# Regrouping the PSUM banks and moving small VectorE work in a fused attention and feed-forward kernel

## The chip, the cores and the metric

The kernel runs on one core of a Trainium2 chip. The metric is the device time of one launch in microseconds (us). The kernel before takes 555.98 us, the median of nine runs (555.08 to 556.79).

The engines are TensorE (PE in the profile; its weight loads have a row of their own, PEld), VectorE (DVE), ScalarE (ACT), GpSimd (POOL) and SyncE (SP, which here only issues transfers). TensorE writes its results to PSUM, which this kernel divides into eight banks of 512 fp32 columns on 128 partitions. DVE and ACT bring them from there to SBUF.

## The reference

The inputs are q, k and v of 8 batches, 12 heads, 448 tokens and 64 dimensions, a gain g of 768, and the weights w1 (768 x 3072) and w2 (3072 x 768).

```
scores = q @ k.T / sqrt(64)
attn   = max(scores, 0)**2 / 448
x      = attn @ v                       # 8 x 448 x 768 after the heads are joined
mu, var over the 768 columns
xn     = (x - mu) / sqrt(var + 1e-6) * g
out    = x + max(xn @ w1, 0) @ w2       # float32
```

## The kernel before

**Order of work.** The order of every engine's queue is the order of the program text (`tc.manual_schedule`), so what stands ahead of an instruction in the text on the same engine also runs ahead of it. First comes the attention of batch 0 (`step_fine`, `first_end`). Then, for each batch, `ffn_1_all(b)` (24 tiles of 128 hidden columns, `ffn_1`) and FFN2: `ffn_2_first` for batch 0, `ffn_2_all` for the others. The attention of batch b + 1 is woven into the feed-forward of batch b: in FFN1 of batch 0 by `step_a` and `step_b` at every second tile, afterwards by `excursion`, which takes three score slots of work at each tile of `IN_FFN1` (the AV product of a finished pair of heads, three times QK with ReLU, three squares), and by `between` inside FFN2.

**Attention.** `att_T` makes the transposes of q and k of a pair of heads, on TensorE for batches 0 and 1, by transfers later. `att_QK` multiplies k by q for the two heads of a pair (two matmuls with 64 rows each, one per half of a two-bank slot) and applies the ReLU: ACT for most, DVE for the third one of an excursion (`relus=(2,)`, L229). `att_square` squares on DVE (L236). `att_AV` (L250) multiplies by v into one bank, which L260 (DVE) or L258 (ACT) empties into xT.

**Mean and gain.** LayerNorm is applied as xc = g x - g mean, and the division by the standard deviation comes at the end. `gain` (L276, ACT) makes g x; `center` makes the mean with four matmuls (L282), two on xs (the sum of the first five column blocks) and two on the last block of xT, and subtracts it with six DVE instructions (L288).

**FFN1.** `ffn_1` runs twelve matmuls into one of two f banks (`next_f` gives them in turn, also to AV in FFN1), and ACT applies the ReLU into h (L324). `h` holds 640 columns: the 448 of this batch at the right (from CARRY = 192), and to their left the tokens that the batch before left over, because FFN2 works on pairs of 128-token tiles. `carry(b)` (L336, DVE) copies these leftover columns from the right end of h to the left, after the last pair. From tile 16 or 18 on, `ffn_stats` computes mean and variance of a token tile on DVE at every second tile.

**FFN2.** Batch 0 multiplies two token tiles plainly (`plain_part`, L370), with four output pieces in turn in the f banks; after each, DVE writes the scaled result (`scaled_plus`, L356). The other batches use Strassen's seven products for each pair of tiles (`seven`, L387): products c, d, a, c, d, a, and c again, in three banks. With `s_sb` (L381) DVE forms the sums of h, with `w2_sums` (L178) the sums of w2, in two halves each. `flush` emits the evacuations of a product after the next product. Batches 1, 2, 3, 5, 6 and 7 have two pairs, batch 4 has one; with one pair the first bank is z, with two it is x and z is the second.

**PSUM before.** Three slots of two banks (`sc`) and two f banks. One score slot is always held back from the turns: slot 0 in the attention of batch 0 (warm-up matmuls and the third tile of `ffn_1_first` in one bank, the first mean in the other), and in FFN2 the slot that has been unused longest, whose halves are the bank z and the bank for AV. In FFN1 all three turn; the TensorE transposes from pair 7 on and the mean of `center` take a half of the next slot.

```
x_bank = f_turn.items[0]
y_bank = f_turn.items[1]
z_bank, av_bank = hold[:, 0], hold[:, 1]
...
banks = [x_bank, z_bank, y_bank] if len(pairs) == 2 else [z_bank, x_bank, y_bank]
```

Of the kernel before, what the change touches and what calls it, by code (L numbers as in the profile page):

```python
# [11 lines left out]
def kernel(  # L12
# [10 lines left out]
    nc = tc.nc  # L23
    P = 128
# [3 lines left out]
    Alu = mybir.AluOpType  # L28
# [55 lines left out]
    v_ring = big_pool.tile([SP, NPAIR, 2, NJ * D], bf16)  # L84

    sc = []
    for n in range(3):
        sc_t = ps_pool.tile([P, 2, 512], fp32, name=f"sc{n}")
        sc.append(sc_t)
    fb = []  # L90
    for n in range(2):
        f_t = ps_pool.tile([P, 512], fp32, name=f"f{n}")
        fb.append(f_t)

# [3 lines left out]
    class Turns:  # L98
        def __init__(self, items):
            self.items = list(items)  # L100

        def next(self, skip=()):
            n = next(n for n, it in enumerate(self.items) if not any(it is s for s in skip))
            it = self.items.pop(n)
            self.items.append(it)
            return it

    sc_turn = Turns(sc)
    f_turn = Turns(fb)
    held = [sc[0]]  # L110

    def next_sc():
        return sc_turn.next(held)

    next_f = f_turn.next

    PE_T = 2
    EARLY = H * NJ * D
# [81 lines left out]
    def att_T(i, copy=None):  # L200
        if i >= PE_T * NPAIR:
            new_qkT(i)
            for t in range(2):
                nc.sync.dma_start_transpose(
                    qkT[i][:, t, :].rearrange("p (j s) -> p j s", j=NJ), qk_ring[:, i % 3, t])
            return
        if i == 0:
            new_qkT(0)
            for t, cp in enumerate((nc.vector.tensor_copy, nc.scalar.copy)):
                ps = bf_view(next_f())  # L210
                pe_T(0, t, ps)
                cp(qkT[0][:, t, :], ps[:, t, :])
            return
        ps = bf_view(next_f() if i <= NPAIR else next_sc()[:, 0])
        for t in range(2):
            pe_T(i, t, ps)
        new_qkT(i)
        (copy or nc.vector.tensor_copy)(qkT[i], ps)  # L218

    def att_QK(i, t, square=True, relu_by=None):  # L220
        at = attn_pool.tile([SP, 2, S], bf16, tag="attn")
        attn[i, t] = at
        ps = next_sc()
        for hh in range(2):
            r = slice(hh * D, (hh + 1) * D)
            nc.tensor.matmul(ps[:SP, hh, :S], qkT[i][r, 1, t * SP:(t + 1) * SP], qkT[i][r, 0, :],  # L226
                             start=True, stop=True)
        if relu_by is nc.vector:
            nc.vector.tensor_scalar(at, ps[:SP, :, :S], 0.0, None, op0=Alu.max)  # L229
        else:  # L230
            nc.scalar.activation(at, ps[:SP, :, :S], Act.Relu)  # L231
        if square:
            att_square(i, t)
# [33 lines left out]
        elif 1 < pr < NPAIR - 1:  # L267
            nc.vector.tensor_add(xs, xs, xT_of(b, pr))

    mean0 = sc[0][:, 1, :S]  # L270

    def mean_part(ki):
        nc.tensor.matmul(mean0, ones, xT_of(0, ki), start=(ki == 0), stop=(ki == K1 - 1))
# [2 lines left out]
        nc.scalar.activation(xc[:, ki, :], xT_of(b, ki), Act.Identity, scale=g_sb[:, ki:ki + 1])  # L276

    def center(b):
        mean_ps = next_sc()[:, 0, :S]
        for n, part in enumerate((xs, xT_of(b, K1 - 1))):  # L280
            for c in range(2):
                nc.tensor.matmul(mean_ps[c * D:(c + 1) * D, :], ones[:, :D], part,  # L282
                                 start=(n == 0), stop=(n == 1))
        for ki in range(K1):
            center_part(ki, mean_ps)
# [37 lines left out]
                                 start=(ki == 0), stop=(ki == K1 - 1))  # L323
        nc.scalar.activation(h[:, ni, CARRY:], ps, Act.Relu)  # L324


    done_to = [0]

    def h_cols(b, m):
        c0 = CARRY + m * P - b * S  # L330
        return slice(c0, c0 + P)

    def carry(b):
        n = (b + 1) * S - done_to[0] * P
        if n:
            nc.vector.tensor_copy(h[:, :, CARRY - n:CARRY], h[:, :, HW - n:])  # L336

    def new_o():
        o_t = o_pool.tile([P, HD], fp32, tag="o")
# [58 lines left out]
    def seven(b, pair, banks, last, between):  # L398
# [63 lines left out]
            between(n)  # L462
        if last:
            cut = HD - P
            parts = ((bb, 0, cut), (sc[0][:, 1], cut, HD))
            for ps, d0, d1 in parts:
                product(ps, sums[6], B_TOP, True, d0, d1)
                flush()

                def after(ps=ps, d0=d0, d1=d1):  # L470
                    o_t = new_o()[:, :d1 - d0]
                    scaled_plus(o_t, ps[:, :d1 - d0], m2, acc2[:, d0:d1])
                    store(o_t, m2, HD + d0, HD + d1, (nc.sync, nc.scalar))
                posts.append(after)
            flush()

    def warm_up(n):
        for _ in range(n):
            nc.tensor.matmul(sc[0][:, 0, :256], ones, warm, start=True, stop=True)

    NP_ALL = B * NPAIR

# [79 lines left out]

    def ffn_1_first():
        f_ps, m_ps = next_f(), next_f()
        tiles = [t[:, :S] for t in (f_ps, m_ps, sc[0][:, 0])]
        for ki in range(K1):
            center_part(ki, mean0)
            for ni, ps in enumerate(tiles):
                nc.tensor.matmul(ps, w1[:, ki, ni * P:(ni + 1) * P], xc[:, ki, :],  # L569
                                 start=(ki == 0), stop=(ki == K1 - 1))  # L570
        for ni, ps in enumerate(tiles):
            nc.scalar.activation(h[:, ni, CARRY:], ps, Act.Relu)
        for t in range(2):
            att_square(NPAIR, t)
        held.clear()

    def second_steps():
        yield lambda: step_b(NPAIR)
# [4 lines left out]
    def ffn_1_all(b):  # L583
        steps = second_steps() if b == 0 else None
        ms = tiles_of(b)
        for ni in range(3 if b == 0 else 0, K2):
            if b == 0 and ni == 3:
                ffn_1_first()
            if 3 <= ni < 3 + K1:
                ffn_x(b, ni - 3)  # L590
            ffn_1(ni)
            flush()
            m = (ni - (K2 - 2 * len(ms))) // 2
            if m >= 0 and ni % 2 == 0:
                ffn_stats(ms[m])
            if b == 1 and ni in (1, 3):
                w2_sums(B12, B12, B22, Alu.subtract, ni // 2)
                w2_sums(B21, B21, B11, Alu.subtract, ni // 2)
            if b == 0 and ni % 2 == 1:
                next(steps)()  # L600
            if 0 < b < B - 1 and ni in IN_FFN1[b]:
                excursion(3, relus=(2,))
        assert steps is None or next(steps, None) is None

    ONE = [b for b in range(B) if ((b + 1) * S // (2 * P)) - (b * S // (2 * P)) == 1]
    IN_FFN1 = {b: (1, 4, 7, 10, 13, 16, 19, 22) if b in ONE else (2, 5, 8, 11, 14, 17, 20)
               for b in range(B)}

    def ffn_2_first():
        b = 0  # L610
        ffn_rstd(b)
        box = {}
        n = 0
        for dh in range(2):
            for m in range(2):
                for part in range(4):
                    plain_part(b, m, dh, part, 4, box)
                    if n == 1:
                        att_AV(PE_T * NPAIR - 1)
                    if n < K1 - 1:  # L620
                        gain(1, n)
                    if n == 3:
                        gain(1, K1 - 1)
                    if n == 4:
                        gain(1, K1 - 2)
                        center(1)
                    if n >= 9 and n < 15:
                        slot, x, y = ((B_SUM, B11, B22), (B_TOP, B11, B12), (B_BOT, B21, B22))[(n - 9) // 2]
                        w2_sums(slot, x, y, Alu.add, (n - 9) % 2)
                    n += 1  # L630
        done_to[0] = 2
        carry(b)

    def ffn_2_all(b):
        ffn_rstd(b)
        hold = sc_turn.items[0]
        held.append(hold)
        x_bank = f_turn.items[0]
        y_bank = f_turn.items[1]
        z_bank, av_bank = hold[:, 0], hold[:, 1]  # L640
        first = done_to[0] // 2
        pairs = range(first, (b + 1) * S // (2 * P))
        banks = [x_bank, z_bank, y_bank] if len(pairs) == 2 else [z_bank, x_bank, y_bank]
        gains = list(range(K1)) if b < B - 1 else []
# [1 line left out]

        def between(n):
            n += 7 * (pr - first)
            if b == B - 1:
                return  # L650
            if slots_left():
                if n in (1, 3):
                    excursion(min(2, slots_left()), av_bank, nc.scalar)
            elif ready:
                att_AV(ready.pop(0), bank=av_bank, evac_by=nc.scalar)
            done = (b + 2) * NPAIR - len(ready) - NPAIR * (b + 1)
            done -= sum(1 for i, t in slots if t == NJ - 1 and i < (b + 2) * NPAIR)
            for _ in range(2):
                if gains and gains[0] < done:
                    gain(b + 1, gains.pop(0))  # L660
            if not gains and not centered[0]:
                center(b + 1)
                centered[0] = True
# [4 lines left out]
        for pr in pairs:  # L668
            last = b == B - 1 and pr == pairs[-1]
            seven(b, pr, banks, last, between)  # L670
            banks = banks[1:] + banks[:1]
            if pr == pairs[-1]:
                done_to[0] = 2 * (pairs[-1] + 1)
                carry(b)
        assert centered[0] and not gains
        held.clear()

    E = mybir.EngineType
    ENGINES = [E.PE, E.Pool, E.DVE, E.Activation, E.SP]
# [62 lines left out]
```

## Time and profile before

| | |
|---|---|
| median of nine runs | 555.98 us |
| the profiled execution | 555.8 us, its span 553.8 us |
| DVE L336, the carry copies | 6 instructions, 5.7 us |
| DVE L178, the sums of w2 | 10 instructions, 13.0 us, mean 1353 ns |
| DVE L229, ReLU of the third score | 43 instructions, 46.8 us, mean 1088 ns |
| DVE L260, emptying AV | 37 instructions, 22.8 us, mean 617 ns |
| TensorE L226, the scores | 384 matmuls, 54.6 us |

The span is the time from the first to the last instruction of one profiled execution; the time of the execution holds some 2.0 us more. In the lines of the timeline the columns are the start, the duration, the engine, the line of the kernel, the operation, the tile written and the tile read, their shapes, and how many instructions are merged; in brackets stands the idle time of the engine before it, with what released it. A row of the waits has the engine, the tile and line that waited, what it waited for, the total in us, how many times, and the longest. Matmul ends are modelled, so the distance from one start to the next says more than a duration.

The stages in this execution: attention of batch 0 to 42 us, FFN1 of batch 0 to 80, its FFN2 to 98, FFN1 of batch 1 to 136, its FFN2 to 168, and so on; FFN2 of batch 4 lies between 341.5 and 358.5 us.

### The profile page before, as it was taken

To read this page: it belongs to the slowest core of one execution; us is meant where nothing else is said; L and a number is where in the kernel's file an instruction comes from. 1 tells how busy PE (TensorE), PEld (TensorE's weight loads), DVE (VectorE), ACT (ScalarE), POOL (GpSimd) and SP (SyncE) were. 2 spreads that over 40 slices of the span, in tenths; PEclk is the share of its full clock that TensorE was granted. 3 is DMA by queue.
4 is the path that set the end of the run, shared out by engine and by line. 5 is a ranking of instruction groups with operands and counts; after the bars stand their busy time and mean duration, and the time that the engine had idled before them with its cause. 6 is when DMAs were issued, how large, how long until landed. Compare 5 with 4: busy or idle time off the path is not lost. (4 is left out here: it accounts for less than half of the span.)

```text
span 553.8 us, 13597 instructions
## 1 busy us (share of the span) xinstructions
PE 531.8 (96%) x5729; PEld 342.4 (62%) x5729; DVE 398.7 (72%) x677; ACT 265.9 (48%) x421; POOL 143.9 (26%) x208
## 2 busy tenths in 40 slices
PE   8969999899999999999999999899999999999996
PEld 5425557555676556855568555655568556687785
DVE  4954577979885788847887569857897677960475
ACT  6926781466405664056640665276630766204400
POOL 8222147027400643015520228104720000000000
PEclk9978999999999999999999999999999999999999
DMA  9999999269733985449962479529963310122022
GB/s 165 196 189 207 204 161 163 51 88 118 78 71 84 113 81 61 86 88 106 91 72 83 70 87 122 74 66 94 118 82 84 71 28 2 54 65 52 5 59 58
DMA packets 162988, 51.86 MB, mean 94 GB/s; under 512 B 128752, under 2 KB 162928, under 8 KB 162928
## 3 DMA queue, kind: packets, MB, share of 16 engines
q0 software_dynamic: 94176, 25.74, 49.5%
q1 hardware_dynamic: 68256, 24.86, 22.6%
q8 instruction: 45, 0.74, 0.6%
q10 hardware_dynamic: 496, 0.40, 0.2%
q14 instruction: 15, 0.12, 0.1%
HBM read 51.91 MB, written 11.01 MB: 114 GB/s over the span
## 5 line engine op out<-in xcount | busy, mean ns | idle before, releaser
L322 PE MATMUL f<-xc,w 128*64 128x448 bf16 x2268 | 227.5, 355 | 1.9 <-DVE o_t L356 1.3
L322 PEld LDWEIGHTS <-w 128*64 128x64 bf16 x2268 | 130.5, 110 | 90.8 <-issue 19.8
L324 ACT ACTIVATE h<-f 128x448 bf16<-128x448 f32 x189 | 103.1, 546 | 165.6 <-PE f L322 149.6
L231 ACT ACTIVATE at<-sc 112x896 bf16<-112x896 f32 x149 | 128.1, 916 | 20.1 <-PE sc L226 20.1
L387 PEld LDWEIGHTS <-s_sb 128*64 128x64 bf16 x1584 | 103.6, 110 | 26.1 <-DVE s_sb L381 2.2
L236 DVE TENSOR_TENSOR at<-at 112x896 bf16<-112x896 bf16 x192 | 110.3, 619 | 13.1 <-ACT at L231 12.9
L138 POOL DMA_DIRECT2D qk_ring<-in_q_dram x72 | 50.7, 710 | 218.0 <-DMA qkT_t<-qk_ring 196.9
L387 PE MATMUL f<-w,s_sb 128*64 128x384 bf16 x1080 | 93.0, 326 | 1.2 <-DVE s_sb L381 1.2
L229 DVE TENSOR_SCALAR at<-sc 112x896 bf16<-112x896 f32 x43 | 46.8, 1088 | 27.1 <-PE sc L226 26.9
L381 DVE TENSOR_TENSOR s_sb<-h 128x1536 bf16<-128x1536 bf16 x65 | 60.6, 949 | 0.0
L138 POOL DMA_DIRECT2D qk_ring<-in_k_dram x72 | 50.3, 703 | 20.8 <-DMA w<-in_moe_w_ch_dram 11.3
L226 PE MATMUL sc<-qkT_t 64*112 64x448 bf16 x384 | 54.6, 369 | 0.3 <-DVE qkT_t L218 0.2
L387 PEld LDWEIGHTS <-h 128*64 128x64 bf16 x624 | 40.1, 110 | 16.2 <-issue 5.5
L260 DVE TENSOR_SCALAR xT<-f 128x448 bf16<-128x448 f32 x37 | 22.8, 617 | 34.6 <-PE f L250 21.6
L387 PE MATMUL sc<-w,s_sb 128*64 128x384 bf16 (+2 forms) x504 | 42.9, 319 | 0.2 <-DVE s_sb L381 0.2
L226 PEld LDWEIGHTS <-qkT_t 64*112 64x112 bf16 x384 | 20.0, 125 | 31.9 <-issue 27.2
L288 DVE SCALAR_TENSOR_TENSOR xc<-sc,g_sb,xc 128x448 bf16<-128x448 f32 x48 | 29.6, 680 | 8.3 <-PE sc L569 5.7
L387 PE MATMUL sc<-w,h 128*64 128x384 bf16 x312 | 27.7, 326 | 4.3 <-DVE o_t L356 4.3
L250 PE MATMUL f<-at,v_ring 112*64 112x448 bf16 x248 | 30.0, 355 | 0.0
L387 PE MATMUL f<-w,h 128*64 128x384 bf16 x312 | 27.7, 326 | 0.0
L250 PEld LDWEIGHTS <-v_ring 112*64 112x64 bf16 x336 | 18.2, 109 | 13.4 <-issue 2.9
L276 ACT ACTIVATE xc<-xT,g_sb 128x448 bf16<-128x448 bf16 x43 | 26.2, 667 | 0.4 <-DVE xT L260 0.2
(71 smaller groups left out, 315.7 us busy)
## 6 DMA issues: line engine op xcount, KB each, us to landing
w<-in_moe_w_ch_dram POOLq DMA_DIRECT2D x6, 768.0 KB, 30.9
w<-in_moe_w_ch_dram POOLq DMA_DIRECT2D x4, 1152.0 KB, 36.4
qk_ring<-in_q_dram POOLq DMA_DIRECT2D x72, 56.0 KB, 3.4
qk_ring<-in_k_dram POOLq DMA_DIRECT2D x72, 56.0 KB, 3.8
v_ring<-in_v_dram POOLq DMA_DIRECT2D x36, 112.0 KB, 3.8
out_dram<-o_t SPq DMA_DIRECT2D x9, 168.0 KB, 2.5
out_dram<-o_t SPq DMA_DIRECT2D x9, 144.0 KB, 2.1
x_tok<-xT SPq DMA_TRANSPOSE x72, 2.5
```

The lines of the kernel that those rows point to most:

```text
L138: nc.gpsimd.dma_start(sb[:, :, x, :], src[b, 2 * a + x].rearrange("(p j) d -> p j d", j=NJ))
L226: nc.tensor.matmul(ps[:SP, hh, :S], qkT[i][r, 1, t * SP:(t + 1) * SP], qkT[i][r, 0, :], start=True, stop=True)
L229: nc.vector.tensor_scalar(at, ps[:SP, :, :S], 0.0, None, op0=Alu.max)
L231: nc.scalar.activation(at, ps[:SP, :, :S], Act.Relu)
L236: nc.vector.tensor_mul(attn[i, t], attn[i, t], attn[i, t])
L250: nc.tensor.matmul(ps[hh * D:(hh + 1) * D, :], v_of(i)[:, hh, t * D:(t + 1) * D], attn[i, t][:, hh, :], start=(t == 0), stop=(t == NJ - 1))
L276: nc.scalar.activation(xc[:, ki, :], xT_of(b, ki), Act.Identity, scale=g_sb[:, ki:ki + 1])
L288: nc.vector.scalar_tensor_tensor(xc[:, ki, :], mean_ps, g_sb[:, ki:ki + 1], xc[:, ki, :], op0=Alu.mult, op1=Alu.add)
L322: nc.tensor.matmul(ps[c * D:(c + 1) * D, :], w1[:, ki, n0:n0 + D], xc[:, ki, :], start=(ki == 0), stop=(ki == K1 - 1))
L324: nc.scalar.activation(h[:, ni, CARRY:], ps, Act.Relu)
L381: nc.vector.tensor_tensor(s_sb[:, n], x, y, op=op)
L387: nc.tensor.matmul(ps[c * D:(c + 1) * D, :d1 - d0], stat[:, ki, c * D:(c + 1) * D], w2[:, slot, ki, d0:d1], start=(start and ki == 0), sto ...
```

## The change

PSUM becomes two slots of two banks (sc) and four single banks: two f banks as before, and two more, `spare`. Where DVE applies the ReLU, the scores of the two heads go to spare[0] and spare[1], and DVE reads them with two instructions. The transposes of `att_T` from pair 7 on take the spare banks in turn. The first mean is in spare[0]; the warm-up matmuls, the third tile of `ffn_1_first`, the mean of `center` and the last cut of the last product are in spare[1]; AV within `ffn_2_first` is in spare[0]. In `ffn_2_all`, z is spare[0] and the bank for AV is spare[1], and no slot is held back.

The carry copy is made in two halves of h and inside FFN2: in batch 0 after the ninth of sixteen parts (n = 8), in two-pair batches after the second product of the second pair (n = 8), in batch 4 after the second product (n = 1). The sums of w2: `ffn_2_first` keeps B_SUM (n = 9 and 10) and B_TOP (n = 12 and 13, before at 11 and 12); B_BOT, which stood there at n = 13 and 14, and B12 and B21, which stood at tiles 1 and 3 of FFN1 of batch 1, go to tiles 0, 3, 6, 9, 12 and 15 of it, one half each.

```diff
-    for n in range(3):
+    for n in range(2):
         sc_t = ps_pool.tile([P, 2, 512], fp32, name=f"sc{n}")
...
-    for n in range(2):
+    for n in range(4):
         f_t = ps_pool.tile([P, 512], fp32, name=f"f{n}")
...
+    next_sc = Turns(sc).next
+    f_turn = Turns(fb[:2])
     next_f = f_turn.next
+    spare = fb[2:]
+    next_spare = Turns(spare).next
...
-        ps = bf_view(next_f() if i <= NPAIR else next_sc()[:, 0])
+        ps = bf_view(next_f() if i <= NPAIR else next_spare())
...
-        ps = next_sc()
+        ps = next_sc() if relu_by is not nc.vector else None
         for hh in range(2):
             r = slice(hh * D, (hh + 1) * D)
-            nc.tensor.matmul(ps[:SP, hh, :S], qkT[i][r, 1, t * SP:(t + 1) * SP], qkT[i][r, 0, :],
+            half = spare[hh] if ps is None else ps[:, hh]
+            nc.tensor.matmul(half[:SP, :S], qkT[i][r, 1, t * SP:(t + 1) * SP], qkT[i][r, 0, :],
                              start=True, stop=True)
-        if relu_by is nc.vector:
-            nc.vector.tensor_scalar(at, ps[:SP, :, :S], 0.0, None, op0=Alu.max)
+        if ps is None:
+            for hh in range(2):
+                nc.vector.tensor_scalar(at[:, hh], spare[hh][:SP, :S], 0.0, None, op0=Alu.max)
...
-    mean0 = sc[0][:, 1, :S]
+    mean0 = spare[0][:, :S]
...
-        mean_ps = next_sc()[:, 0, :S]
+        mean_ps = spare[1][:, :S]
...
     def carry(b):
-        n = (b + 1) * S - done_to[0] * P
-        if n:
-            nc.vector.tensor_copy(h[:, :, CARRY - n:CARRY], h[:, :, HW - n:])
+        n = (b + 1) * S % (2 * P)
+        for k0 in range(0, K2 if n else 0, KH):
+            nc.vector.tensor_copy(h[:, k0:k0 + KH, CARRY - n:CARRY], h[:, k0:k0 + KH, HW - n:])
...
-            parts = ((bb, 0, cut), (sc[0][:, 1], cut, HD))
+            parts = ((bb, 0, cut), (spare[1], cut, HD))
...
-            nc.tensor.matmul(sc[0][:, 0, :256], ones, warm, start=True, stop=True)
+            nc.tensor.matmul(spare[1][:, :256], ones, warm, start=True, stop=True)
...
-        tiles = [t[:, :S] for t in (f_ps, m_ps, sc[0][:, 0])]
+        tiles = [t[:, :S] for t in (f_ps, m_ps, spare[1])]
...
-            if b == 1 and ni in (1, 3):
-                w2_sums(B12, B12, B22, Alu.subtract, ni // 2)
-                w2_sums(B21, B21, B11, Alu.subtract, ni // 2)
+            if b == 1 and ni in SUMS_AT:
+                w2_sums(*LATE_SUMS[SUMS_AT.index(ni)])
...
+    SUMS_AT = (0, 3, 6, 9, 12, 15)
+    LATE_SUMS = [(o, x, y, op, part)
+                 for o, x, y, op in ((B_BOT, B21, B22, Alu.add), (B12, B12, B22, Alu.subtract),
+                                     (B21, B21, B11, Alu.subtract)) for part in range(2)]
...
-                        att_AV(PE_T * NPAIR - 1)
+                        att_AV(PE_T * NPAIR - 1, bank=spare[0])
...
-                    if n >= 9 and n < 15:
-                        slot, x, y = ((B_SUM, B11, B22), (B_TOP, B11, B12), (B_BOT, B21, B22))[(n - 9) // 2]
-                        w2_sums(slot, x, y, Alu.add, (n - 9) % 2)
+                    if n == 8:
+                        carry(b)
+                    if n in (9, 10):
+                        w2_sums(B_SUM, B11, B22, Alu.add, n - 9)
+                    if n in (12, 13):
+                        w2_sums(B_TOP, B11, B12, Alu.add, n - 12)
                     n += 1
-        done_to[0] = 2
-        carry(b)
...
-        hold = sc_turn.items[0]
-        held.append(hold)
-        x_bank = f_turn.items[0]
-        y_bank = f_turn.items[1]
-        z_bank, av_bank = hold[:, 0], hold[:, 1]
-        first = done_to[0] // 2
+        x_bank, y_bank = f_turn.items
+        z_bank, av_bank = spare
+        first = b * S // (2 * P)
...
             n += 7 * (pr - first)
+            if n == (8 if len(pairs) == 2 else 1):
+                carry(b)
...
-            if pr == pairs[-1]:
-                done_to[0] = 2 * (pairs[-1] + 1)
-                carry(b)
```

More of the change, by code (lines that the diff above doesn't have):

```diff
@@ L100, in __init__, with next @@
             self.items = list(items)
-        def next(self, skip=()):
-            n = next(n for n, it in enumerate(self.items) if not any(it is s for s in skip))
-            it = self.items.pop(n)
+        def next(self):
+            it = self.items.pop(0)
             self.items.append(it)
             return it
[L108 to L113, printed above, removed]
+    next_sc = Turns(sc).next
+    f_turn = Turns(fb[:2])
     next_f = f_turn.next
+    spare = fb[2:]
+    next_spare = Turns(spare).next
     PE_T = 2
@@ L324, in ffn_1 @@
         nc.scalar.activation(h[:, ni, CARRY:], ps, Act.Relu)
-    done_to = [0]
     def h_cols(b, m):
@@ L574, in ffn_1_first @@
             att_square(NPAIR, t)
-        held.clear()
     def second_steps():
@@ L671, in ffn_2_all @@
             banks = banks[1:] + banks[:1]
-            if pr == pairs[-1]:
-                done_to[0] = 2 * (pairs[-1] + 1)
-                carry(b)
         assert centered[0] and not gains
-        held.clear()
     E = mybir.EngineType
```

## The prediction

> **What bounds it.** I read the page first, then what TensorE waits for, then the timeline around each of those waits.
>
> ```profile
> PE 531.8 (96%) x5729; PEld 342.4 (62%) x5729; DVE 398.7 (72%) x677; ACT 265.9 (48%) x421; POOL 143.9 (26%) x208
> ...
> PE sc L387 <- DVE o_t L356: 4.3, 5, 0.9
> PE sc L282 <- ACT xT L258: 2.2, 5, 0.4
> PE f L322 <- DVE o_t L356: 1.3, 1, 1.3
> ...
> PE f L370 <- DVE o_t L356: 0.7, 1, 0.7
> PE f L322 <- ACT h L324: 0.6, 1, 0.6
> ```
>
> TensorE is busy for 96% of the 553.8 us span, and the change takes no matmul away. So only TensorE's waits can be won or added, and the rows above are the ones that the change touches: three single waits around 85 to 102 us (the end of batch 0) and two that come once in each of the five FFN2 stages with two pairs and a centring (batches 1, 2, 3, 5, 6). VectorE (DVE) at 72% matters only where it is late for TensorE.
>
> I count from start to start, because ends overlap. Twelve L322 matmuls (one ffn_1 tile) take 36 x 0.0978 / 3 = 1.17 us (three tiles run 3.52 in the chain), 24 of L370 or L387 take 1.95, and a DVE instruction holds its engine about 0.08 less than its duration: four weight sums of 1.353 start at 94.59 and the next instruction at 99.66, so 1.27 each.
>
> **End of batch 0: the gain.** In the timeline:
>
> ```profile
> 85.65 1.17 PE L370 MATMUL f<-w,h 128*64 128x384 bf16 x12 [0.71 <-DVE o_t L356]
> ...
> 94.59 5.16 DVE L178 TENSOR_TENSOR w<-w 128x2304 bf16<-128x2304 bf16 x4
> 97.72 1.33 PE L322 MATMUL f<-xc,w 128*64 128x448 bf16 x12
> 99.66 0.61 DVE L356 SCALAR_TENSOR_TENSOR o_t<-f,rstd,x_tok 128x384 f32<-128x384 f32 x1
> 100.19 1.35 DVE L336 COPY h<-h 128x4608 bf16<-128x4608 bf16 x1
> 100.33 1.33 PE L322 MATMUL f<-xc,w 128*64 128x448 bf16 x12 [1.27 <-DVE o_t L356]
> 101.64 0.98 ACT L324 ACTIVATE h<-f 128x448 bf16<-128x448 f32 x2 [16.02 <-DVE h L336]
> 102.23 1.33 PE L322 MATMUL f<-xc,w 128*64 128x448 bf16 x12 [0.58 <-ACT h L324]
> ```
>
> Three stalls in a row. The AV product of the last attention pair takes one of the two f banks, so the second output tile gets the bank of the first and waits for its evacuation. Then six weight sums hold the last evacuation back, so the second ffn_1 tile waits. Then the carry copy holds the first ReLU back, so the third waits.
>
> After: that AV is in spare[0], so the second output tile starts at 82.82 + 1.95 = 84.77 instead of 85.65 (0.88), and the first ffn_1 tile at 96.84. DVE, worked forward: centring 86.42 to 89.98 (3.56 as now), one evacuation (0.52) to 90.50, the carry as two copies. Copies of 1536, 3072 and 4608 elements last 0.55, 0.95 and 1.35, so 2304 lasts 0.75 and holds 0.67: two are 1.34, to 91.84. Two sums to 94.37, an evacuation to 94.90, two sums to 97.43, the last evacuation ends at 98.04. The second ffn_1 tile wants its bank at 96.84 + 1.17 = 98.01, so 0.1 is left of its stall, and the ReLU behind it meets no copy. The third tile starts at 99.28 instead of 102.23: **-2.95**.
>
> **Where the other sums go.** Six sums now stand in FFN1 of batch 1 at tiles 0, 3, 6, 9, 12 and 15. Up to 12 they fit: between excursions DVE idles for about 1.3 (before 122.86, for instance). At 15 they meet the statistics, which start at tile 16:
>
> ```profile
> 126.43 0.55 DVE L313 BATCH_NORM_STATS2 stats<-x_tok 128x6 f32<-128x384 bf16 x1
> ...
> 127.73 1.09 DVE L229 TENSOR_SCALAR at<-sc 112x896 bf16<-112x896 f32 x1
> ...
> 132.61 3.60 PE L322 MATMUL f<-xc,w 128*64 128x448 bf16 x36
> 132.68 0.58 DVE L260 TENSOR_SCALAR xT<-f 128x448 bf16<-128x448 f32 x1
> ```
>
> From 123.5 to 132.7 DVE has no gap over 0.05. So the sum (1.27) and two ReLUs in halves (0.07 each, below) push L260, which empties the AV bank, from 132.68 to 134.05, ending at 134.63. Tile 22 uses that bank next and wants it at 132.61 + 1.17 = 133.78: a new stall, **+0.9**. The queue behind it (xs, ReLU, squares, statistics, rstd, first h sum) then slips 0.5 more than TensorE; that h sum would be ready at about 140.3 against a product at 142.2, so nothing is added.
>
> **The mean in the AV bank.** Centring takes spare[1] instead of a score slot, and in two-pair stages the last AV has just been written there.
>
> ```profile
> 148.39 0.36 PE L282 MATMUL sc<-xs,ones 128*64 128x448 bf16 x2
> 148.60 0.54 ACT L258 ACTIVATE xT<-sc 128x448 bf16<-128x448 f32 x1 [1.91 <-PE sc L250]
> ...
> 149.20 0.38 PE L282 MATMUL sc<-xT,ones 128*64 128x448 bf16 x2 [0.45 <-ACT xT L258]
> 149.65 3.64 DVE L288 SCALAR_TENSOR_TENSOR xc<-sc,g_sb,xc 128x448 bf16<-128x448 f32 x6
> ...
> 154.33 2.14 PE L387 MATMUL sc<-w,h 128*64 128x384 bf16 x24 [0.85 <-DVE o_t L356]
> ```
>
> Today the xs half of the mean runs while ACT empties the AV bank; after, it waits too. [...] By the rows it is far less, since the xT half waits for the same ACT instruction today: only the two xs matmuls move behind it, 0.19 (86.62 to 86.81 in batch 0). [...] TensorE's 0.19 would vanish in the 0.85 wait at 154.33, but DVE's start at 149.65 moves as well (its mean is ready about 0.45 after the xT matmuls start, so 149.84), and that wait ends with DVE's chain. Five times 0.19: **+0.95**; bounds 0 (if DVE has slack there) and 4.1. Batches 0 and 4 centre long after the AV bank is empty: nothing.
>
> **Batch 4, the one-pair stage.** Its first product goes to the z bank, then half of a score slot that ACT emptied long ago, now spare[0], which DVE empties in the last excursion:
>
> ```profile
> 341.68 2.12 PE L387 MATMUL sc<-w,h 128*64 128x384 bf16 x24
> 341.81 1.08 DVE L229 TENSOR_SCALAR at<-sc 112x896 bf16<-112x896 f32 x1
> ```
>
> The bank comes free at about 342.5 (the first half ends at 341.88 + 0.60), so the product starts 0.86 late. Today the AV behind it waits for its last square; 0.33 is given back there, and the next product starts at 345.27 instead of 344.74. Behind the wait stand AV, its evacuation, the gains and the mean, so centring starts 0.53 late and DVE is full from there to the end: **+0.5**, bounds 0.3 and 0.9.
>
> **Costed at nothing.** *ReLU in halves*: 448 elements in L260 last 617 ns, so two hold DVE 2 x 0.54 = 1.08 against 1.01. 43 times 0.07 is 3.0 us of DVE, hidden in its gaps outside the tails counted above; the price without that cover is those 3.0. *Carry within FFN2*: in two-pair stages it falls before L414 (158.53), which DVE waits 0.94 for; 128 columns take 2 x 0.47. Late by 1 us it would still meet h sum 2, needed at 162.13 and ready at 159.95. In batch 4 it takes 1.34 where DVE idles 0.73 and 0.80. Its place at the stage's end held up nothing but batch 0. *Two score slots in FFN1 of batch 0*: steps are 2.9 apart at least, and both slots are empty 0.63 before the next (64.64 and 65.27). *No DMA is moved*: SP, POOL and both load rings keep their orders; loads and stores follow TensorE's times. *Warm-up, first mean, last cut*: other banks, same distances.
>
> **Sum.** -2.95 + 0.9 + 0.95 + 0.5 = -0.6. The profiled execution took 555.8 (553.8 and 2.0 around it), 0.2 under the median of nine, 555.98. Forecast: 555.4.
>
> **Rivals.**
> *The new waits cost next to nothing*: L260's stall and half of the means' delays are absorbed, as waits in a queue often are. For it: the estimates are shares of a microsecond on ends that are modelled. Against it: DVE has no gap before L260. -2.95 + 0.5 + 0.5 = -2.0: 554.0.
> *Score pairs lose their overlap* (slower): the third slot's two matmuls now wait for two releases, and each half signals its own. Two matmuls of such a pair run side by side today (three pairs take 0.70, one takes 0.33, so 0.19 for a pair of 0.37). If the second no longer starts beside the first, each of 43 pays up to 0.19, 8.2 us: 563.6; at a third of that 2.7, 558.1. From 0.04 each, 1.7 us, the kernel is slower by over 0.2%. Against it: the releases are 3 us old by then, and the first matmul of each ffn_1 tile waits for a release today without breaking the 0.0978 rhythm.
> [...]
> *It doesn't do what it says*: the copy inside batch 0's FFN2 could hold products that read h, if the two were tracked as one region. The columns are apart (0 to 191 and 448 to 639 against 192 to 447). Products behind it would wait from about 90.0 to 91.8: 557.2.
>
> **Numbers.** My sum as it stands, with its own range 554.4 to 556.6: 0.50. Waits absorbed: 0.22. Overlap lost: 0.12. Bank rule in full: 0.08. Held by the copy: 0.08. The range is 553.7 to 557.5: it takes in the first two cases and the last, and leaves out most of the two slower ones. A change under 0.2% (1.1 us) can't be told from none here. Below 554.9: most of the absorbed case and a fifth of the sum's, 0.30. Above 557.1: the two slower cases, half of the last and a tail of the sum, 0.26. Between: 0.44.
>
> **What would show it.** Right: no wait at L370, and the third tile of batch 1 about 2.9 earlier; a wait of TensorE at L322 on L260 of 0.5 to 1.2, two tiles before FFN2 of batch 1; L282 waits on L258 as before, but ahead of the xs matmuls, with 0.19 more to the centring; a wait of the first product of batch 4 on DVE's ReLU. Wrong: pairs of L226 in excursions that take longer than 0.70, or a wait of L370 on the copy. A gain over 2 us means that the tail of batch 1 had slack that I didn't see; a loss over 1 us means that a wait repeats in every batch, outside the five means.

## The result and the profile after

| | before | after |
|---|---|---|
| device time, median | 555.81 us (52 runs) | 552.1 us (17 runs) |
| ratio after to before | | 0.9934, interval 0.9919 to 0.9948 |
| span of the profiled execution | 553.8 us | 549.7 us |
| DVE busy, instructions | 398.7 us, 677 | 402.0 us, 726 |

The kernel is 0.66% faster; the forecast was 555.4 us with a range from 553.7 to 557.5, so the sign of the best guess was right and the size was not. In the stretches that the forecast worked out, the kernel after is slower (below), so the sign came out right for a reason that the forecast doesn't have: by luck. In the kernel after, lines have moved: L387 is now L384, L370 L367, L356 L353, L226 L225, L569 L566, L178 L176, L349 L346 and L204 L202.

What TensorE waits for in the kernel after, from the waits of its profile (total, times, longest):

```profile
PE f L384 <- DVE o_t L353: 4.5, 5, 0.9
PE f L322 <- DVE o_t L353: 3.6, 1, 3.6
PE f L282 <- ACT xT L258: 3.2, 5, 0.6
...
PE f L566 <- DVE xc L288: 0.8, 1, 0.8
PE f L384 <- DVE at L229: 0.7, 1, 0.7
PE f L322 <- DVE xT L260: 0.6, 1, 0.6
```

Two rows are strange to the forecast. The wait of L566 for the centring (L569 before, 4.7 us in six waits) is down to one of 0.8, and a wait of 3.6 us on an output tile has appeared. To see what each did, both profiled executions are divided at the same instructions, and the difference of each stretch stands beside what the forecast has for it:

| from ... to | before | after | difference | forecast |
|---|---|---|---|---|
| start ... first centring instruction (L288) | 31.27 | 30.33 | -0.94 | 0 |
| ... first L322 matmul | 11.11 | 4.68 | -6.43 | 0 |
| ... first product of FFN2, batch 0 | 37.73 | 36.62 | -1.11 | 0 |
| ... first scores in FFN1 of batch 1 | 23.38 | 25.01 | +1.63 | -2.95 |
| ... first product of FFN2, batch 1 | 32.55 | 33.95 | +1.40 | +0.9 |
| ... first product of FFN2, batch 4 | 205.64 | 207.21 | +1.57 | +1.43 |
| ... end | 212.12 | 211.90 | -0.22 | +0.02 |
| sum | 553.8 | 549.7 | -4.10 | -0.6 |

(The last forecasts are three means of 0.19 and the 0.86 late start of batch 4, then two means and what batch 4 gives back.) The first row isn't the change: in the ten profiles here the first centring starts between 30.3 and 32.4 us, earlier or later whatever the edit. The second and third rows are the gain, 7.54 us, and the forecast has nothing there. The four rows below them, for which it has -0.6 in all, lost 4.38.

The second row is `ffn_1_first`. Its timeline before (start, duration):

```profile
32.01 0.54 PE L569 MATMUL f<-xc,w 128*128 128x448 bf16 x2 [0.78 <-DVE xc L288]
32.38 0.35 PE L569 MATMUL sc<-xc,w 128*128 128x448 bf16 x1
32.78 0.68 DVE L288 SCALAR_TENSOR_TENSOR xc<-sc,g_sb,xc 128x448 bf16<-128x448 f32 x1 [0.82 <-PE sc L569]
33.51 0.54 PE L569 MATMUL f<-xc,w 128*128 128x448 bf16 x2 [0.78 <-DVE xc L288]
...
37.07 0.90 PE L569 MATMUL f<-xc,w 128*128 128x448 bf16 x2 [0.78 <-DVE xc L288]
...
39.12 0.90 PE L569 MATMUL f<-xc,w 128*128 128x448 bf16 x2 [0.78 <-DVE xc L288]
...
42.38 2.43 PE L322 MATMUL f<-xc,w 128*64 128x448 bf16 x12
```

and after:

```profile
30.33 3.64 DVE L288 SCALAR_TENSOR_TENSOR xc<-f,g_sb,xc 128x448 bf16<-128x448 f32 x6
31.07 3.69 PE L566 MATMUL f<-xc,w 128*128 128x448 bf16 x18 [0.78 <-DVE xc L288]
...
35.01 1.33 PE L322 MATMUL f<-xc,w 128*64 128x448 bf16 x12 [0.25 <-ACT h L569]
```

Before, the two engines take turns: TensorE waits 0.78 for a centred column block, and DVE waits 0.82 for TensorE before it centres the next. The first wait is data, since TensorE multiplies the block. The second is not: DVE reads the mean and needs nothing from the third tile. But the mean was `sc[0][:, 1]` and the third tile `sc[0][:, 0]`, two banks of one tile. After, they are two tiles, and six centrings and 18 matmuls run side by side.

The instructions in the trace carry the semaphores that each waits for (the counters by which one engine tells another that it is done), and they say the same. Before, all six centrings of batch 0 wait for TensorE, the last also for DVE. After, the first alone waits for TensorE, the next four wait for nothing and the last for DVE.

The third row is the clock that TensorE was granted. The table by stretches of the kernel before has, after the busy times of the engines, this clock as a share of full speed. It falls to a half while the engines take turns, and recovers only in the first L322 tiles:

```profile
31.00:34.40 3.40, 1.69 (x7) 0.57 (x6) 1.69 (x4) 1.36 (x2) 0.00 (x0) 1.00 1.48 175
34.40:37.80 3.40, 2.01 (x6) 0.68 (x6) 1.25 (x2) 0.00 (x0) 1.02 (x1) 0.50 1.35 195
37.80:41.20 3.40, 1.85 (x6) 0.54 (x5) 1.44 (x3) 0.00 (x0) 1.01 (x1) 0.50 1.25 206
41.20:44.60 3.40, 3.40 (x15) 1.12 (x14) 0.99 (x2) 1.42 (x3) 0.72 (x1) 0.50 1.24 206
44.80:48.20 3.40, 3.40 (x48) 1.94 (x48) 1.78 (x3) 2.75 (x5) 0.71 (x1) 1.00 1.24 208
```

The first L322 tile then takes 2.36 us (42.38 to the scores at 44.74) against 1.25 after (35.01 to 36.26), where the clock is 1.00 in both stretches: 1.11, the whole third row.

The clock is in the second row as well. A turn takes 1.50 us at full clock (32.01 to 33.51) and 2.05 at half (37.07 to 39.12). Three turns and the last three matmuls ran at half. An estimate: 3 x 0.55 for the turns, 0.5 for these matmuls (two take 0.37 us at full clock, 32.01 to 32.38, and 0.70 at half, 41.18 to 41.88) and 1.11 for the tile, so 3.3 of the 7.54 us are clock and the rest are the turns themselves. How much clock is lost differs between executions of one kernel. Of the 41 of the kernel before that were timed with the experiments, four had a mean clock of 0.999 or 1.000; they took 551.96 to 552.79 us, some 3.3 under the median. Of the 17 after, six had 1.000; they took 550.08 to 551.11. So at full clock the change gains about 2 of the 3.7 us. No trace of the kernel before at full clock was kept, so this division stays an estimate.

The fourth row is where the forecast's own gain was lost: +1.63 instead of -2.95, 4.58 us apart. After:

```profile
77.97 9.23 SPq L202 DMA_TRANSPOSE qkT_t<-qk_ring  x5
...
87.30 6.73 SPq L346 DMA_DIRECT2D out_dram<-o_t  x8
...
92.60 0.62 DVE L353 SCALAR_TENSOR_TENSOR o_t<-f,rstd,x_tok 128x384 f32<-128x384 f32 x1 [3.41 <-DMA out_dram<-o_t]
...
93.27 3.44 PE L322 MATMUL f<-xc,w 128*64 128x448 bf16 x24 [3.60 <-DVE o_t L353]
```

The fourth output piece of batch 0 needs the buffer of the first (there are three), and the store of the first stands on SP behind the transposes for batch 2. These wait for q and k, whose loads on POOL (L136) wait 27.2 us in all for the loads of the weights. The loads hardly became earlier with TensorE: FFN2 of batch 0 starts 8.48 us earlier than before (71.63 against 80.11), the last of these transposes ends only 1.70 earlier (87.21 against 88.91). The kernel runs into them.

### The profile page after: what moved, and what is told of

The parts are those of the page before. It is cut to its first block, busy times and chain, and to the rows that moved or that the text cites. A ratio compares the mean times of both kernels' runs of the same rounds, so it can differ in the third digit from the quotient of the medians.

```text
span 549.7 us, 13638 instructions
## 1 busy us (share of the span) xinstructions
PE 528.9 (96%) x5729; PEld 342.0 (62%) x5729; DVE 402.0 (73%) x726; ACT 266.3 (48%) x421; POOL 144.9 (26%) x208
## 4 chain that ended last, share of the span: by engine, by line
PE 72%; DMA 15%; DVE 7%; POOL 3%; ACT 1%; issue 1%; SPq 0%; POOLq 0%; DVEq 0%
PE f L322 33%; PE f L384 28%; DMA w<-in_moe_w_ch_dram 7%; DMA s_sb<-in_v_dram 5%; PE f L250 5%; PE sc L225 4%; DVE xc L288 4%; DMA qkT_t<-qk_ring 1%; PE f L225 1%; POOL w L127 1%; DMA qk_ring<-in_k_dram 1%; DMA out_dram<-o_t 1%; DVE o_t L353 1%; POOL qk_ring L136 1%; ACT xc L276 1%
## 5 line engine op out<-in xcount | busy, mean ns | idle before, releaser
L322 PE MATMUL f<-xc,w 128*64 128x448 bf16 x2268 | 227.4, 355 | 4.5 <-DVE o_t L353 3.6
L322 PEld LDWEIGHTS <-w 128*64 128x64 bf16 x2268 | 131.0, 110 | 92.8 <-issue 21.5
L384 PE MATMUL f<-w,s_sb 128*64 128x384 bf16 (+2 forms) x1584 | 131.8, 324 | 1.4 <-DVE s_sb L378 1.4
L384 PEld LDWEIGHTS <-s_sb 128*64 128x64 bf16 x1584 | 103.7, 110 | 26.2 <-DVE s_sb L378 2.2
L136 POOL DMA_DIRECT2D qk_ring<-in_q_dram x72 | 50.7, 710 | 215.7 <-DMA qkT_t<-qk_ring 195.4
L229 DVE TENSOR_SCALAR at<-f 112x448 bf16<-112x448 f32 x86 | 49.5, 618 | 30.9 <-PE f L225 30.8
L384 PE MATMUL f<-w,h 128*64 128x384 bf16 x624 | 53.3, 326 | 5.2 <-DVE o_t L353 4.5
L136 POOL DMA_DIRECT2D qk_ring<-in_k_dram x72 | 51.3, 717 | 17.9 <-DMA w<-in_moe_w_ch_dram 11.3
L384 PEld LDWEIGHTS <-h 128*64 128x64 bf16 x624 | 41.1, 110 | 16.4 <-issue 6.6
L225 PE MATMUL sc<-qkT_t 64*112 64x448 bf16 x298 | 46.8, 378 | 0.3 <-DVE qkT_t L216 0.2
L260 DVE TENSOR_SCALAR xT<-f 128x448 bf16<-128x448 f32 x37 | 22.8, 617 | 30.3 <-PE f L250 20.7
L250 PE MATMUL f<-at,v_ring 112*64 112x448 bf16 x336 | 40.3, 354 | 0.0
L225 PEld LDWEIGHTS <-qkT_t 64*112 64x112 bf16 x384 | 20.1, 126 | 31.9 <-issue 27.1
L288 DVE SCALAR_TENSOR_TENSOR xc<-f,g_sb,xc 128x448 bf16<-128x448 f32 x48 | 29.1, 677 | 2.2 <-PE f L282 1.5
L408 ACT COPY acc<-f 128x384 f32<-128x384 f32 x13 | 6.1, 470 | 48.8 <-PE f L384 35.0
L141 POOL DMA_DIRECT2D v_ring<-in_v_dram x36 | 24.7, 690 | 7.9 <-DMA w<-in_moe_w_ch_dram 5.1
```

The lines of the kernel that those rows point to most:

```text
L136: nc.gpsimd.dma_start(sb[:, :, x, :], src[b, 2 * a + x].rearrange("(p j) d -> p j d", j=NJ))
L225: nc.tensor.matmul(half[:SP, :S], qkT[i][r, 1, t * SP:(t + 1) * SP], qkT[i][r, 0, :], start=True, stop=True)
L229: nc.vector.tensor_scalar(at[:, hh], spare[hh][:SP, :S], 0.0, None, op0=Alu.max)
L250: nc.tensor.matmul(ps[hh * D:(hh + 1) * D, :], v_of(i)[:, hh, t * D:(t + 1) * D], attn[i, t][:, hh, :], start=(t == 0), stop=(t == NJ - 1))
L288: nc.vector.scalar_tensor_tensor(xc[:, ki, :], mean_ps, g_sb[:, ki:ki + 1], xc[:, ki, :], op0=Alu.mult, op1=Alu.add)
L322: nc.tensor.matmul(ps[c * D:(c + 1) * D, :], w1[:, ki, n0:n0 + D], xc[:, ki, :], start=(ki == 0), stop=(ki == K1 - 1))
```

## The experiments

Theory A: the gain is the separation of the mean and the third tile, and what it brings. Theory B: the gain is what the forecast listed for the end of batch 0. Times are medians; ratios are to the kernel before in the same runs, with a 95% interval in brackets.

**One tile again.** The kernel after, its two spare banks declared as one tile:

```diff
-    for n in range(4):
+    for n in range(2):
...
+    sp_t = ps_pool.tile([P, 2, 512], fp32, name="spares")
+    fb += [sp_t[:, 0], sp_t[:, 1]]
```

> The kernel after, with the two spare banks declared as one tile of two banks instead of two tiles; banks, order and work are the same. Theory A: the centring of batch 0 again waits for TensorE five times (about 5.7 us in all), FFN1 of batch 0 starts at about 42 instead of 35 us, the 3.6 us wait of L322 for an output store vanishes, and the total is about that of my forecast, 555 to 556, or more if z and the AV bank also hold each other up. Theory B: no difference from the changed kernel, 551.5 to 552.5.

Measured: 560.47 us, ratio 1.0088 (1.0063 to 1.0114), slower than before. Its waits of DVE and of TensorE (its lines stand two further down than in the kernel after):

```profile
DVE xc L290 <- PE spares L568: 5.7, 5, 1.4
...
PE f L568 <- DVE xc L290: 4.7, 6, 0.8
PE spares L386 <- DVE xc L290: 3.7, 1, 3.7
```

The five waits of 5.7 us in all are back, exactly as before the change, and so is TensorE's semaphore in all six centrings; the first centring to the first main tile takes 11.11 us again (30.88 to 41.99), and the store wait is gone. No matmul is added or moved in the program; only how the banks are declared differs. The third row is new, and most of why it is worse than before: in batch 4 the z product must now wait 3.7 us for six centrings that read the other bank of its tile, the clock is at 0.50 for 6.9 us around and behind it, and from the first product of batch 4 to the end it takes 217.03 us instead of 212.12. So the total alone decides little; the stretches do. With the late start back, the end of batch 0 (the fourth row of the table) takes 20.37 us, 3.01 under before: the forecast's own gain is there as well, where the kernel after has lost it. Theory A stands; B falls as the source of the gain of the kernel after.

**The separation alone.** The kernel before, with one line:

```diff
-        tiles = [t[:, :S] for t in (f_ps, m_ps, sc[0][:, 0])]
+        tiles = [t[:, :S] for t in (f_ps, m_ps, sc_turn.items[1][:, 0])]
```

> The kernel before, with one edit: the third tile of the first FFN1 goes to a half of another score slot, so that it no longer shares a two-bank tile with the first mean. Theory A (the gain of the change comes from that sharing: each centring instruction waits for the third tile's matmul and each group of matmuls for the centring): the stretch from the first centring instruction to the first L322 matmul falls from 11.1 to about 4.7 us, the first L322 tile from 2.4 to 1.25, so FFN1 of batch 0 starts about 7.5 earlier; of this the output stores of batch 0 may take back 0.5 to 2. Total 547.5 to 550. Theory B (the gain comes from the bank for AV, the copy and the sums, as forecast, and the earlier start is a lucky profile): 555 to 556.5, no change.

Measured: 551.14 us, ratio 0.9924 (0.9898 to 0.9949), which is the whole gain of the change within the interval. The stretch is 4.68 us (31.34 to 36.02), as after, and of the six centrings only the first waits for TensorE. The total is 1.1 us above the range expected: the store wait is larger here than after, and the clock behind it stays at 0.50 for longer (last section):

```profile
95.07 0.62 DVE L356 SCALAR_TENSOR_TENSOR o_t<-f,rstd,x_tok 128x384 f32<-128x384 f32 x1 [2.79 <-DMA out_dram<-o_t]
...
95.74 4.69 PE L322 MATMUL f<-xc,w 128*64 128x448 bf16 x24 [4.15 <-DVE o_t L356]
```

**A fourth output buffer.** The kernel after, with

```diff
-    o_pool = ctx.enter_context(tc.tile_pool(name="o", bufs=3))
+    o_pool = ctx.enter_context(tc.tile_pool(name="o", bufs=4))
```

> The kernel after, with four output buffers instead of three. Theory A1 (the end of batch 0 now waits for the landing of an output store, which stands on SP behind transposes that wait for loads): the 3.6 us wait of L322 vanishes, and with it about 1 us of slower matmuls after the pause: 547.5 to 549. Rival A2 (the loads bound the whole stretch, so TensorE waits for the next transposes instead): within 1 us of the changed kernel, 551 to 552.5.

Measured: 548.55 us, ratio 0.9888 (0.9854 to 0.9922), 3.5 under the changed kernel. The wait is gone, and the stretch from the first product of batch 0 to the first scores in FFN1 of batch 1 is 20.37 us (73.42 to 93.79) against 23.38 before: -3.01, where the forecast has -2.95. So A1, and the loads give room for it.

**The forecast's part alone.** The kernel before with its PSUM, and of the change only the AV bank, the copy in two halves and the spread of the sums (in part; the other batches still copy at the end of their stage):

```diff
-                        att_AV(PE_T * NPAIR - 1)
+                        att_AV(PE_T * NPAIR - 1, bank=next_sc()[:, 0])
...
+                    if n == 8:
+                        carry(b)
+                    if n in (9, 10):
+                        w2_sums(B_SUM, B11, B22, Alu.add, n - 9)
+                    if n in (12, 13):
+                        w2_sums(B_TOP, B11, B12, Alu.add, n - 12)
...
+    SUMS_AT = (0, 3, 6, 9, 12, 15)
```

> The kernel before with its PSUM, and only this of the change: the AV of the last pair in a score slot, the copy inside FFN2 as two halves (batch 0 at n = 8, elsewhere at the end as before), the sums spread over FFN1 of batch 1. If my working of that stage holds for the times at which it was made: -2.95 at the third tile of batch 1, +0.6 to +0.9 at tile 22, no wait for a store, total 553.4 to 554. If the store wait belongs to the edits themselves and not to the earlier start: 556 or more.

Measured: 552.84 us, ratio 0.9953 (0.9934 to 0.9972), 3.2 under the kernel before and 0.6 better than the range expected. The same stretch is 20.67 us (82.53 to 103.20), so -2.71; TensorE waits 0.5 for L260, a little less than expected, and no store holds it. (The profiled execution as a whole took 555.81 us: it lost more clock in `ffn_1_first`, ahead of that stretch: 13.7 us at 0.50 where the kernel before has 10.2.) The edits are worth about what the forecast says, as long as nothing behind them holds the stores up; with four buffers (above) they are worth it in the early start too.

**The sum at tile 15.** The kernel after, with

```diff
-    SUMS_AT = (0, 3, 6, 9, 12, 15)
+    SUMS_AT = (0, 1, 3, 6, 9, 12)
```

> The kernel after with the sums of w2 at tiles 0, 1, 3, 6, 9 and 12 instead of 0, 3, 6, 9, 12 and 15. My step says that the sum at tile 15 delays L260 and costs TensorE 0.6 (measured) to 0.9 (forecast): the wait of L322 on L260 vanishes, total 551.3 to 551.7 against 552.1. If the wait has another cause, it stays.

Measured: 551.81 us, ratio 0.9918 (0.9887 to 0.9949): by time it can't be told from the changed kernel. Its profile has no wait of L322 on L260 any more, and the stretch from the first scores of batch 1 to its FFN2 takes 32.94 us instead of 33.95 (of which 1.37, 96.64 to 98.01, are at half clock), so the cause is the one named. In the kernel after it is this:

```profile
127.69 0.58 DVE L260 TENSOR_SCALAR xT<-f 128x448 bf16<-128x448 f32 x1
...
128.32 2.46 PE L322 MATMUL f<-xc,w 128*64 128x448 bf16 x24 [0.62 <-DVE xT L260]
```

**The mean in a score slot.** The kernel after, with

```diff
-        mean_ps = spare[1][:, :S]
+        mean_ps = next_sc()[:, 0, :S]
```

> The kernel after with the mean of center in a score slot instead of the bank of the last AV. My step: five times 0.19, the xs half runs again before ACT has emptied the bank, the wait at the second pair stays near 0.85, total about 551.2. [...] If DVE has slack there: no change.

Measured: 550.96 us, ratio 0.9907 (0.9877 to 0.9936), 1.1 under the changed kernel in the medians, with intervals that overlap. The wait of L282 is 2.2 us in five again instead of 3.2. The forecast's upper bound for the mean, 4.1 us, is excluded by the traces: from one two-pair FFN2 to the next the kernel before takes 68.02 us and the kernel after 68.25, 0.23 more.

**The combinations.** The kernel after with four output buffers, no sum at tile 15 and the mean in a score slot, and the kernel before with the separation, the forecast's part (without tile 15) and four output buffers.

> The kernel after with four output buffers, the sums of w2 at tiles 0, 1, 3, 6, 9 and 12 (none at 15), and the mean of center in a score slot as before. On the changed kernel with four buffers (548.55) this should take off the wait of tile 22 for L260 (0.6) and five times 0.19 of the later mean: 546.5 to 547.5. If these waits are absorbed elsewhere: 548 to 549.

> The PSUM of the kernel before (three two-bank slots, two f banks), with the third tile in another slot, the AV of the last pair in a score slot, the copy and the sums of batch 0 spread (none at tile 15) and four output buffers. If regrouping the banks is worth nothing beyond the one separation, this equals the combination on the changed kernel or beats it by the 0.7 that batch 4 loses there: 546 to 547.5. If the single banks are worth more than that: 1 us or more above it.

Measured: 545.69 us, ratio 0.983 (0.9792 to 0.9867), and 544.90 us, ratio 0.9802 (0.9777 to 0.9828). Both beat the changed kernel by over 6 us, and both are a little under the range expected. In the profile of the second, the stretches of the second, third and fourth row are 4.67, 36.62 and 20.39 us: the two gains add. The two kernels can't be told apart by time. Their spans, 543.6 and 542.9 us, differ by 0.7, but so do the starts of their first centring (31.24 and 30.56), which the edits don't touch. The first still has the 0.7 us wait of batch 4 (L384 on L229), which the second can't have. So no gain of two slots and four single banks over three slots shows in these five runs of each, once the mean and the third tile are apart. Of the second, what TensorE still waits for longest:

```profile
PE sc L387 <- DVE o_t L356: 4.3, 5, 0.9
PE sc L282 <- ACT xT L258: 2.2, 5, 0.4
PE sc L479 <- DVE w L96: 1.2, 1, 1.2
PE f L387 <- DVE s_sb L381: 1.2, 1, 1.2
PE f L569 <- DVE xc L288: 0.8, 1, 0.8
```

## Why the prediction was wrong

**The failing step** is the choice of rows: "only TensorE's waits can be won or added, and the rows above are the ones that the change touches". The largest row of that view is not among them, nor is DVE's counterpart:

```profile
PE f L569 <- DVE xc L288: 4.7, 6, 0.8
...
DVE xc L288 <- PE sc L569: 5.7, 5, 1.4
```

The change does touch it, since it moves the first mean and the third tile from one tile to two. The forecast put that at nothing: "Warm-up, first mean, last cut: other banks, same distances" (the third tile isn't named). The pair of rows looks like a data dependence, and one of its two directions is one; the other came with the declaration. The gain is 6.43 us in that stretch, a third of it clock by the estimate above, and 1.11 behind it, all clock. The forecast also said that a gain over 2 us would mean slack in the tail of batch 1. The gain was 3.7, and that tail got slower.

**"No DMA is moved"** failed with it: "loads and stores follow TensorE's times". They do not: SP's queue holds the stores behind transposes that follow the loads, and these follow the weights. With FFN2 of batch 0 8.48 us earlier and the last of these transposes only 1.70, the queue's order mattered: 3.60 us of waiting, and 3.37 instead of 2.35 us for the two tiles behind it. Without these two the stretch after the change would have been 25.01 - 3.60 - 1.02 = 20.39 us, 2.99 under before, so the -2.95 was right for the times for which it was made. With four buffers the last four rows of the table come to -3.01, +0.75, +1.57 and +0.56, -0.13 in all where the forecast has -0.6: the rest of the working nearly holds.

**Tile 22 of batch 1**, +0.9 forecast: 0.62 measured, by the mechanism named (the forecast's own terms give 134.09 for L260, not 134.05). The other 0.8 of that stretch is mostly the first excursion, which takes 4.84 us instead of 4.23 (103.49 to 107.72 before, 96.64 to 101.48 after), since the clock is at 0.50 until 98.0.

**The mean**, +0.95: right in mechanism, 0.23 rather than 0.19 for a stage. No run shows the 4.1 us that the forecast has as upper bound and as the case "Bank rule in full" (0.08): five times 0.23 is 1.15.

```profile
143.77 0.38 PE L282 MATMUL f<-xs,ones 128*64 128x448 bf16 x2 [0.64 <-ACT xT L258]
143.96 0.38 PE L282 MATMUL f<-xT,ones 128*64 128x448 bf16 x2
144.45 3.64 DVE L288 SCALAR_TENSOR_TENSOR xc<-f,g_sb,xc 128x448 bf16<-128x448 f32 x6
...
149.13 4.09 PE L384 MATMUL f<-w,h 128*64 128x384 bf16 x48 [0.89 <-DVE o_t L353]
```

Both mean halves now run behind ACT, DVE starts 0.49 after the second, and the wait at the second pair stays.

**Batch 4**, +0.5: its first product waits 0.70 for the first ReLU half, and from it to the first tile of batch 5 the kernel takes 16.61 us instead of 16.96, so 0.35 is given back.

**What else was costed at nothing** held: the 86 ReLU halves of 618 ns cost DVE 2.7 us (49.5 against 46.8), and TensorE has no wait for them outside the stretches named; FFN1 of batch 0 takes 36.62 us with two score slots and, with the separation alone, 36.62 with three; no row of TensorE's waits has the copies (L333). Of the rivals, the lost overlap of score pairs did not happen (three pairs at full clock still take 0.71 us, 101.48 to 102.19), nor did the copy hold products.

## What to carry to other kernels

In this program a PSUM tile of two banks was one object to the waits: what read one bank waited for what wrote the other (DVE waited 5.7 us in five waits for the third tile before, and again with one tile, and not once after). Declare banks as separate tiles unless one instruction uses both, or keep what must not wait for each other out of one tile. Before a wait in a profile is believed, ask what data it carries; where two engines wait for each other in turn and one of the waits carries none, a declaration may remove both.

When a stage starts earlier, look at each queue that it now meets sooner, here the stores behind transposes on SP: a gain of 7.54 us upstream was taken back in part by a wait of 3.60, until a fourth buffer gave it room.

## What the runs showed of the hardware

In the kernel after, the wait of 3.60 us cost TensorE more than its length: the clock fell behind it. With four buffers this wait is gone, and the clock is 1.00 from 86 to 95. The kernel after, around the wait, which ends at 93.27:

```profile
91.20:94.60 3.40, 1.33 (x15) 0.98 (x16) 1.88 (x2) 0.00 (x0) 2.79 (x4) 1.00 1.77 218
94.60:98.00 3.40, 3.40 (x20) 1.47 (x18) 0.00 (x0) 1.79 (x3) 0.00 (x0) 0.50 0.87 130
98.00:101.40 3.40, 3.40 (x38) 1.89 (x36) 3.36 (x6) 2.12 (x4) 0.00 (x0) 1.00 0.27 56
```

The clock falls 1.3 us after the pause is over, when TensorE is busy again, and the two tiles behind it take 3.37 us instead of 2.35. With the separation alone, after a wait of 4.15 us, it is 0.50 from 94.9 to 101.7, and two tiles take 4.6 us instead of 2.35. The kernel after with the mean in a score slot waits 2.54 us at the same place, and its clock stays at 1.00; so it does in the kernel before after 1.27. The shortest single wait behind which the clock fell is 3.46, in the run without a sum at tile 15. Where between 2.54 and 3.46 the change comes, and whether the length alone decides, the runs don't show.

In `ffn_1_first` of the kernel before the clock fell with no wait of TensorE longer than 0.8 us: TensorE was busy for 1.69 of the 3.40 us (31.00 to 34.40) ahead of the fall, and for 2.01 and 1.85 of 3.40 in the next two stretches, at 0.50. In the kernel after it was busy for 3.33 of the 3.40 us from 31.00 to 34.40, and the clock was 1.00 there and in the next 3.40.

Inside the kernel the clock of these traces is 1.00 or 0.50 and nothing between, and the stretches at 0.50 last about 3.4 us or a multiple of it: 3.4 in the kernel after, 6.8 with the separation alone, 10.2 and 6.9 with one tile, 10.2 before, 13.7 with the forecast's part alone. What sets this length, the runs don't show.
